# Forgetting attention with a gated feed-forward block: queries and keys of the first four pairs loaded in two parts, under a new load plan

## The chip, the cores and the metric

One core of a Trainium2 chip runs the whole program. The metric is the time of one execution in microseconds (us), as the device measures it; lower is better. A profile of one such execution stands beside it. Its engines are named as in the profile: PE (TensorE; PEld for its weight loads), DVE (VectorE), ACT (ScalarE), POOL (GpSimd), SP (SyncE, which issues transfers here). An engine's name with a q (SPq) is its queue of instructions that are not counted as busy, such as the issue of a transfer.

## The reference

Eight batches, eight heads, 576 positions of 64 numbers. Attention with a learned decay comes first, then a gated feed-forward block (FFN below) over the 4608 tokens:

```python
scores = scale * np.matmul(q, k.transpose(0, 1, 3, 2))          # 8 x 8 x 576 x 576
cum = np.cumsum(np.log(np.clip(f, 0.0001, 1.0)), axis=-1)
scores = np.where(causal, -1e9, scores + cum[..., :, None] - cum[..., None, :])
attn = np.exp(scores - np.max(scores, axis=-1, keepdims=True))
attn = attn / (np.sum(attn, axis=-1, keepdims=True) + 1e-09)
x = (attn @ v)  # as (4608, 512), heads side by side
g = x @ w_gate                                                  # 512 x 1536
return ((g / (1 + np.exp(-g))) * (x @ w_val)) @ w_out           # 1536 x 512
```

Inputs and output are float32. The kernel multiplies in bf16.

## The kernel before

**Pairs.** Two heads of one batch make a pair; there are 32, four to a batch. For a pair, k and q are loaded (L409), cast to bf16 (L434 to L438, on ACT, DVE or POOL), transposed on PE (L452) and copied out of PSUM into `kt` and `qz` (L464 on ACT, L466 on DVE); the copies below are named by these lines. `qz` holds a block of 64 rows of both heads beside zeros, so that one matmul makes 128 rows: 64 of each head.

**Groups.** The nine blocks of 64 rows of a pair are worked off in two groups: g0 is blocks 0 to 3 (rows 0 to 255), g1 is blocks 4 to 8. Group g0 needs only the first 256 rows of q and k. For each block PE makes scores (L498) and adds the causal mask (L502); DVE adds the summed gates `cb` and takes a row minimum (L526: "the add" below); ACT takes the exponential with its row sum (L546); the reciprocal is L564; POOL multiplies by it (L582). For the first eight pairs PE transposes the result (L612) and DVE or ACT copies it (L617); for later pairs a transposing transfer does that. PE multiplies with v (L638), and ACT or DVE copies the result into `xT` (L662), a ring of 2560 tokens.

**Gate sums.** `f` is loaded for all 64 heads (tile `t`, L364), clamped, its logarithm taken, and summed along the row by a DVE scan (L369). The sums are written to DRAM (`cum_f`, L378), and for each pair two transfers read two rows back, each spread over 64 partitions (L418, `cb`). Only pair 0 (`NSEL = 1`) gets its sums without DRAM: a float32 matmul with a 0/1 matrix `one` spreads them (L393, two halves of 288 columns), and ACT or DVE copies them (L397).

**FFN.** Tokens are taken in tiles of 256, 256, then seven of 512, then 256, 128, 128. For a tile, PE computes gate and value (L720) in units; a unit fills two PSUM banks. ACT takes tanh (L726), DVE multiplies twice (L728, L731). The tiles of 256 tokens have six units of 2 x 8 matmuls of 256 columns. The output projection is L748. Units are taken in a fixed order, so unit 0 of tile 0 needs the weight pieces wg0 and wv0, unit 1 wg2 and wv2, units 2 and 3 wg4 and wv4, units 4 and 5 wg8 and wv8 (the number is the first block of 128 columns that the piece holds). A tile needs `xT` of all four pairs of its batch for its tokens: tile 0 the g0 of pairs 0 to 3, tile 1 their g1, tile 2 the last rows of batch 0 and most of batch 1 (pairs 4 to 7).

**Order.** A planner in Python runs while the program is built. It lists every operation with a cost, an engine or a choice of engines and a priority, simulates the engines, and emits the operations in the order of their simulated starts; every engine then works through its queue in that order. `COLD` is the simulated time in ns up to which PE work is costed at double. `HEAD` gives the first units of work as pair and group; each later pair runs g1, then g0. `STARTUP` is the order of the first transfers, written by hand: `p2` stands for k and q of pair 2, `c2` for its gate sums from DRAM, `f9` for f, `v01` for piece 1 of v of batch 0 (128 rows of all heads), `wg4` for a weight piece (issued by POOL, cast on the way). Each entry waits for the landing of the one `AHEAD` places before it. `NUDGE` shifts priorities of single pairs, tiles or loads (`a4.1:1`: scores of pair 4, g1, later by one).

Of the kernel before, what the change touches and what calls it, by code (L numbers as in the profile page):

```python
# [13 lines left out]

BIG = 1.0e9
HUGE = 3.0e38
COLD = 25000
SLOW = 1.03


# [179 lines left out]
def kernel(  # L200
# [11 lines left out]
    nc = tc.nc  # L212
# [32 lines left out]
    JFROM = 8  # L245
    TWO = True
    NDIRECT = 0
    NSEL = 1
    MOST = (("p", 1), ("o", 2), ("f", 3))
    AHEAD = 7  # L250
    BEHIND = 6
    BOTH = 8
    LATER = {"DVE": 100}
# [3 lines left out]
    SOON = 8  # L257
    BACK = 4
    CBACK = 5
    STARTUP = "p0 f9 p1 c1 p3 p2 c2 v00 c3 wv0 wg2 wg0 wv2 v04 wv4 v01 v03 c4 wg4 v02 p4 wg8 wv8 v10 f0 p5 p6 c5 v14 c6 wo0 p7 wo4 v12 v13 v11 c7 wo8"  # L260
    HEAD = "10 00 20 30 11 01 31 21"


    NUDGE = "a10.0:1 a13.0:2 a15.0:-1 a15.1:-0.5 a16.1:-2 a20.0:-1 a21.0:1 a23.1:-1 a26.1:0.5 a27.1:-1.5 a28.0:1 a29.0:1 a31.1:10 f3:-4 f4:-7 f5:1 f6:2 f7:4.5 f8:4 f9:8 o6:-2.5 o8:2 q11:-2 q15:4 q22:5.5 q24:2.5"

    WAIT = ""
    ORDER = [(int(u[0]), int(u[1])) for u in HEAD.split()]
# [10 lines left out]
    def bufs(name, shape, dtype, n, space=None):  # L278
        pl.pool(name, [(space or sb).tile(shape, dtype, name=f"{name}{x}") for x in range(n)])
# [16 lines left out]
    bufs("qz", [P, NB, 2, QB], BF16, 4)  # L296
    bufs("cb", [P, S], F32, 5)
    bufs("t", [P, S], F32, 4)
    bufs("cm", [P, NB, QB], F32, 2)
# [7 lines left out]
    for n in ("pk", "pT"):  # L307
        both[n] = [sb.tile([P, sum(NSL), P], BF16, name=f"{n}{x}") for x in range(2)]
        pl.pool(n + "1", [x[:, 0:NSL[1], :] for x in both[n]])
        pl.pool(n + "0", [x[:, NSL[1]:, :] for x in both[n]])  # L310
    bufs("vf", [P, H, D], F32, 2)
    bufs("vt", [P, 5, H, D], BF16, 2)
    bufs("th", [P, 512], F32, 3)
    bufs("hh", [P, 512], BF16, 18)
# [21 lines left out]
    one = sb.tile([BH, 2 * max(NSEL, 1), 64], F32)  # L336
    setup({"POOL": 160 + 110 * NSEL}, lambda e: nc.gpsimd.tensor_copy(one, ident[0:BH, 0:2 * max(NSEL, 1)].unsqueeze(2).to_broadcast((BH, 2 * max(NSEL, 1), 64))),
          ["one"], -140)
    setup({"DVE": 100}, lambda e: nc.vector.memset(tiny, 1.0), ["tiny"], -300)
    pl.op({"ACT": 1400}, lambda e: nc.scalar.activation(tiny[:, 1:2], tiny[:, 0:1], AF.Ln), ["tiny"], ["ln"], -99.85)  # L340
# [33 lines left out]
    for p in range(NDIRECT):  # L374
# [5 lines left out]
    pl.op({"ACT": 1400}, lambda e: nc.scalar.activation(tiny[:, 1:2], tiny[:, 0:1], AF.Exp),  # L380
          [(("cb", p), 2) for p in range(NDIRECT)] + [("fa", 2), "ln"], ["exp"], -95)


    def select(p):
        pl.key(("cb", p), "cb", p)
        for n in range(2):
            a, z = S // 2 * n, S // 2 * (n + 1)
            bk = ("cs", p, n)
            pl.key(bk, "gv", line="c")

            def mult(e, p=p, bk=bk, a=a, z=z):
                w = one[:, 2 * p:2 * p + 2, :].rearrange("b h r -> b (h r)")
                nc.tensor.matmul(pl.buf(bk)[:, 0:z - a], w, pl.buf("fa")[0:BH, a:z], start=True, stop=True)  # L393
            pl.op({"PE": mm(4 * (z - a))}, mult, [("fa", 3), "one"], [bk], -98.5 + 3 * p, lat=220, holds=["fa"])

            def evac(e, p=p, bk=bk, a=a, z=z):
                (nc.scalar.copy if e == "ACT" else nc.vector.tensor_copy)(pl.buf(("cb", p))[:, a:z], pl.buf(bk)[:, 0:z - a])  # L397
            pl.op({"ACT": 370, "DVE": 385}, evac, [bk], [("cb", p), (("cb", p), 3)], -98.5 + 3 * p)

    def half(key):  # L400
        return pl.buf(key).bitcast(BF16)
# [2 lines left out]
    def load_pair(p):  # L404
        b, hp = divmod(p, NPB)
        s = first[p]
        for name, src, pr in (("k", k, 0), ("q", q, .1)):
# [5 lines left out]
        if NDIRECT <= p < NSEL:  # L413
            select(p)
        elif p >= NSEL:
            pl.key(("cb", p), "cb", p)
            for h in range(2):
                loads["cb", p, h] = pl.op({"SP": 600}, lambda e, h=h: nc.sync.dma_start(  # L418
                    out=pl.buf(("cb", p))[64 * h:64 * h + 64, :],
                    in_=cum_dram[2 * p + h:2 * p + h + 1, :].to_broadcast((64, S))),  # L420
                    ["cum_dram"], [("cb", p), (("cb", p), 3)], -98.5 + 3 * p if p < NPB else s - SOON + .2, dma=570, after=[sums[p - CBACK, 0 if p - CBACK >= NPB else 1]] if p >= NPB + 1 else [])

    def prepare(p):
        s = first[p]
        for name in ("k", "q"):
            fk, bk = (name + "f", p), (name + "b", p)
            KR, KC = ROWS[name]
            pl.key(bk, name + "b")

            def cast(e, name=name, fk=fk, bk=bk, KR=KR):  # L430
                src = pl.buf(fk)[0:KR, :, :].rearrange("p h (r d) -> p r h d", d=D)
                dst = pl.buf(bk)[0:KR, :, :, :]
                if e == "ACT":
                    nc.scalar.activation(dst, src, AF.Copy, scale=-scale if name == "q" else 1.0)  # L434
                elif name == "q":
                    eng[e].tensor_scalar(dst, src, -scale, 1.0, op0=ALU.mult, op1=ALU.mult)  # L436
                else:
                    eng[e].tensor_copy(dst, src)  # L438
            engs = {"POOL": 850 if p < 8 else 800 if name == "k" else 1010}
            if p < NPB:  # L440
                engs = {"POOL": 850, "ACT": 850, "DVE": 500} if name == "k" else {"POOL": 1050, "ACT": 1050, "DVE": 680}
            o = pl.op(engs, cast, [fk], [bk], s - 1 + (name == "q") * .1)
            o.bias = SPARE if p else {}
            tk = ("tt", name, p)
            pl.key(tk, "tx", line="q")
            ok = ("kt", p) if name == "k" else ("qz", p)
            pl.key(ok, ok[0])

            def transpose(e, bk=bk, tk=tk, KR=KR, KC=KC):
                src = pl.buf(bk).rearrange("p r h d -> p r (h d)")  # L450
                for j in range(KC):
                    nc.tensor.transpose(half(tk)[:, KR * j:KR * j + KR], src[0:KR, j, :], ident[0:KR, 0:KR])  # L452
            pl.op({"PE": KC * (KR / 2.4 + 2.5)}, transpose, [bk], [tk, ok], s - 1, lat=200)
            halves = [(0, P, None)] if name == "k" else [(0, 64, 0), (64, 128, 1)]
            for a, z, h in halves:
                def evac(e, a=a, z=z, h=h, tk=tk, ok=ok, KC=KC):
                    if h is None:
                        src = half(tk)[a:z, 0:S].rearrange("r (j p) -> r p j", j=KC)
                        dst = pl.buf(ok)[a:z, :].rearrange("r (p j) -> r p j", j=KC)
                    else:  # L460
                        src = half(tk)[a:z, 0:S].rearrange("r (j i p) -> r i p j", j=KC, i=NB)
# [6 lines left out]
                o.bias = LATER if p >= 8 else {}  # L468

    def epool(i):  # L470
        return f"e{i}" if i % 2 == 0 else "eo"

# [12 lines left out]
    def scores(p, g):  # L485
# [3 lines left out]
        for n, bank in enumerate(BANKS[g]):  # L489
# [11 lines left out]
                    if last and p < MFROM:  # L501
                        nc.tensor.matmul(sp[:, o - QB:o], ident, mask, start=False, stop=True)  # L502
            cols = [z - a for _, a, z in bank] + [64 for i, a, z in bank if z == QB * (i + 1) and p < MFROM]
            pl.op({"PE": mm(*cols)}, mult, [("kt", p), ("qz", p), (("kt", p), "done"), (("qz", p), "done"), "mask"], [sk], pr, lat=220)
            o = 0
            cuts = []
            for i, a, z in bank:
# [5 lines left out]
            for i, a, z in cuts:  # L513
# [265 lines left out]
    for x in STARTUP.split():  # L779
        n = int("".join(c for c in x if c.isdigit()))  # L780
        if x == "f9":
            line.append(loads["f", "fa", 0])
        elif x[0] == "f" and n < NDIRECT:
            line += [loads["f", ("cb", n), h] for h in range(2)]
        elif x[0] == "p":
# [84 lines left out]
```

## Time and profile before

| | |
|---|---|
| time, three runs | 419.38, 420.01 (median), 426.64 us |
| the profiled execution, its own time | 420.02 us |
| its span, first to last instruction | 418.2 us |
| PE busy | 398.1 us (95%) |
| DVE, ACT, POOL busy | 325.3, 311.0, 252.6 us (78%, 74%, 60%) |
| moved by DMA | 72.22 MB, mean 173 GB/s |

Busy time counts an engine's own instructions. A matmul's end is modelled, so a busy PE need not be a PE at its peak. The time outside the span is 420.02 - 418.2 = 1.8 us. A chain of waits is followed back from the last instruction, at each step to whatever released it. A window view gives the busy time of each engine in one stretch, with the number of its instructions as x. Sizes of transfers in the profile are those at the destination: 288 KB for k or q of a pair, 144 KB for a `cb` half or for f, 256 KB for a full piece of v, 256 or 512 KB for a weight piece.

### The profile page before, as it was taken

To read this page: it belongs to the slowest core of one execution; us is meant where nothing else is said; L and a number is where in the kernel's file an instruction comes from. 1 tells how busy PE (TensorE), PEld (TensorE's weight loads), DVE (VectorE), ACT (ScalarE), POOL (GpSimd) and SP (SyncE) were. 2 spreads that over 40 slices of the span, in tenths; PEclk is the share of its full clock that TensorE was granted. 3 is DMA by queue.
4 is the path that set the end of the run, shared out by engine and by line. 5 is a ranking of instruction groups with operands and counts; after the bars stand their busy time and mean duration, and the time that the engine had idled before them with its cause. 6 is when DMAs were issued, how large, how long until landed. Compare 5 with 4: busy or idle time off the path is not lost.

```text
span 418.2 us, 9999 instructions
## 1 busy us (share of the span) xinstructions
PE 398.1 (95%) x3304; PEld 231.8 (55%) x3304; DVE 325.3 (78%) x1044; ACT 311.0 (74%) x875; POOL 252.6 (60%) x460
## 2 busy tenths in 40 slices
PE   1679999999999999999999999999999999999996
PEld 1446887665555555555555555555454444447875
DVE  4589999989998979889998979898866474553532
ACT  4689999999999978888987979899886332223321
POOL 7399977999788983886795787759784000000000
PEclk9999999999999999999999999999999999999999
DMA  7999999997999999999999999979976401001111
GB/s 176 203 166 235 220 214 206 224 236 183 204 229 212 232 197 237 204 237 199 225 216 226 228 235 210 234 189 208 221 155 146 88 2 51 25 27 50 52 52 52
DMA packets 143029, 72.22 MB, mean 173 GB/s; under 512 B 117761, under 2 KB 129793, under 8 KB 142977
## 3 DMA queue, kind: packets, MB, share of 16 engines
q1 hardware_dynamic: 136804, 66.27, 73.8%
q0 software_dynamic: 5808, 4.72, 7.7%
q10 hardware_dynamic: 364, 0.59, 0.6%
q8 instruction: 26, 0.43, 0.4%
q14 instruction: 27, 0.21, 0.2%
HBM read 47.04 MB, written 9.58 MB: 135 GB/s over the span
## 4 chain that ended last, share of the span: by engine, by line
PE 77%; DMA 7%; ACT 6%; POOL 4%; DVE 3%; issue 2%; SPq 0%; POOLq 0%; DVEq 0%; ACTq 0%
PE gv L720 38%; PE gv L748 20%; PE sp L498 8%; PE tx L638 5%; DMA kf<-in_k_dram 3%; PE tx L452 3%; POOL pk L582 3%; PE gv L612 2%; DMA pT<-pk 2%; DVE t L526 2%; ACT eo L546 2%; ACT e L546 2%; PE sp L502 1%; DMA cb<-cum_f 1%; DMA cum_f<-t 1%
## 5 line engine op out<-in xcount | busy, mean ns | idle before, releaser
L526 DVE CUSTOM_DVE_ANT_0 t<-sp,cb 128x512 f32<-128x512 f32 (+7 forms) x288 | 130.9, 475 | 13.5 <-PE sp L502 5.0
L582 POOL TENSOR_SCALAR pk<-e,lr 128x128 bf16<-128x128 f32 (+3 forms) x190 | 100.1, 530 | 32.7 <-DVE lr L564 15.1
L720 PE MATMUL gv<-xT,wv 128*128 128x512 bf16 (+2 forms) x576 | 111.4, 326 | 0.0
L720 PE MATMUL gv<-xT,wg 128*128 128x512 bf16 (+2 forms) x576 | 111.3, 326 | 0.0
L728 DVE SCALAR_TENSOR_TENSOR th<-th,gv 128x512 f32<-128x512 f32 x108 | 73.9, 685 | 43.7 <-ACT th L726 43.2
L748 PE MATMUL gv<-wo,hh 128*128 128x512 bf16 (+1 forms) x444 | 107.5, 374 | 0.0
L726 ACT ACTIVATE th<-gv 128x512 f32<-128x512 f32 x108 | 64.0, 592 | 42.1 <-PE gv L720 40.3
L546 ACT ACTIVATE e<-t,tm 128x448 f32<-128x448 f32 (+4 forms) x160 | 88.5, 555 | 4.6 <-DVE tm L526 3.9
L731 DVE TENSOR_TENSOR hh<-th,gv 128x512 bf16<-128x512 f32 x108 | 73.4, 685 | 9.0 <-PE gv L720 5.5
L498 PE MATMUL sp<-kt,qz 128*128 128x448 bf16 (+6 forms) x320 | 72.8, 295 | 3.8 <-DVE tm L526 3.7
L582 POOL TENSOR_SCALAR pk<-eo,lr 128x256 bf16<-128x256 f32 (+3 forms) x128 | 67.7, 530 | 12.4 <-DVE lr L564 4.9
L546 ACT ACTIVATE eo<-t,tm 128x256 f32<-128x256 f32 (+3 forms) x128 | 71.2, 557 | 4.3 <-DVE tm L526 2.2
L720 PEld LDWEIGHTS <-wv 128*128 128x128 bf16 x576 | 49.3, 98 | 34.8
L720 PEld LDWEIGHTS <-wg 128*128 128x128 bf16 x576 | 49.2, 98 | 35.0
L748 PEld LDWEIGHTS <-hh 128*128 128x128 bf16 x444 | 39.7, 98 | 37.1
L502 PE MATMUL sp<-mask,ident 128*128 128x64 bf16 x288 | 48.2, 197 | 0.0
L755 ACT ACTIVATE ot<-gv 128x512 f32<-128x512 f32 (+1 forms) x33 | 19.1, 581 | 36.7 <-PE gv L748 34.7
L498 PEld LDWEIGHTS <-qz 128*128 128x128 bf16 x320 | 31.0, 101 | 19.8 <-DVE qz L466 1.3
L436 POOL TENSOR_SCALAR qb<-qf 72x1024 bf16<-72x1024 f32 x30 | 31.2, 1041 | 8.8 <-DMA qf<-in_q_dram 6.1
L502 PEld LDWEIGHTS <-ident 128*128 128x128 bf16 x288 | 27.2, 100 | 15.2 <-issue 3.9
L546 ACT ACTIVATION_READ_ACCUMULATOR e<-t,tm 128x1 f32 x160 | 30.7, 192 | 0.0
L638 PE MATMUL tx<-pT,vt 128*64 128x320 bf16 (+4 forms) x448 | 29.4, 266 | 0.7 <-DMA pT<-pk 0.3
(60 smaller groups left out, 379.7 us busy)
## 6 DMA issues: line engine op xcount, KB each, us to landing
out_dram<-ot SPq DMA_DIRECT2D x35, 256.0 KB
kf<-in_k_dram SPq DMA_DIRECT2D x31, 288.0 KB
qf<-in_q_dram SPq DMA_DIRECT2D x31, 288.0 KB
cb<-cum_f SPq DMA_DIRECT2D x62, 144.0 KB
vf<-in_v_dram SPq DMA_DIRECT2D x32, 256.0 KB
wo<-in_moe_w_out_dram POOLq DMA_DIRECT2D x3, 512.0 KB, 9.2
vf<-in_v_dram SPq DMA_DIRECT2D x8, 128.0 KB
wv<-in_moe_w_val_dram POOLq DMA_DIRECT2D x2, 512.0 KB, 8.3
```

Source lines behind the costliest of these rows:

```text
L436: eng[e].tensor_scalar(dst, src, -scale, 1.0, op0=ALU.mult, op1=ALU.mult)
L498: nc.tensor.matmul(sp[:, o:o + z - a], qz[:, i, :, :].rearrange("p h r -> p (h r)"), kt[:, a:z], start=True, stop=not last or p >= MFROM)
L502: nc.tensor.matmul(sp[:, o - QB:o], ident, mask, start=False, stop=True)
L526: nc.vector.tensor_tensor_reduce(out=pl.buf(tk)[:, a:z], in0=pl.buf(sk)[:, o:o + z - a], in1=pl.buf(("cm", p))[:, i, :] if own else pl.buf ...
L546: nc.scalar.activation(pl.buf(ek)[:, :L], pl.buf(tk)[:, :L], AF.Exp, bias=pl.buf(("tm", p, g))[:, 0, i:i + 1], scale=-1.0, accum_out=pl.bu ...
L582: eng[e].tensor_scalar(dst, src, r, 1.0, op0=ALU.mult, op1=ALU.mult)
L638: nc.tensor.matmul(xo[r, 0:QB * n], vt[:, c, 2 * hp + h, :], pT[:, a:a + n, 64 * h:64 * h + 64], start=(c == 0), stop=(c == nch - 1))
L720: nc.tensor.matmul(pl.buf(bk)[:, j * n:j * n + n], wt[:, ko, fc * P:fc * P + P], xT[:, ko, x0:x0 + n], start=ko == 0, stop=ko == KD - 1)
L726: pl.op({"ACT": 487}, lambda e, u=u: nc.scalar.activation(pl.buf(("th", t, u)), pl.buf(("wg", t, u)), AF.Tanh, scale=0.5), [("wg", t, u)], ...
L728: pl.op({"DVE": 605}, lambda e, u=u: nc.vector.scalar_tensor_tensor(pl.buf(("th", t, u)), pl.buf(("th", t, u)), 1.0, pl.buf(("wg", t, u)), ...
L731: pl.op({"DVE": 605}, lambda e, u=u: nc.vector.tensor_mul(pl.buf(("hh", t, u)), pl.buf(("th", t, u)), pl.buf(("wv", t, u))), [("u", t, u), ...
L748: nc.tensor.matmul(pl.buf(bk)[:, 0:z - a], hh[:, (fc % nf) * n + ms * P:(fc % nf) * n + ms * P + P], wo[:, fc, a:z], start=fc == 0, stop=f ...
```

## The change

- For the first four pairs (`NHALF = 4`) q and k come in parts. Part A is rows 0 to 255 of two pairs together (pairs 0 and 1, pairs 2 and 3), on 128 partitions, 64 for each pair: one cast and four transposes of 128 columns for both. Part B is rows 256 to 575: k for two pairs together (128 partitions, five transposes), q for each pair alone (80 partitions, four transposes). Each pair's share is a transfer of its own. The copies out of PSUM are made for each pair and part. The part A transfers of pairs 0 and 1 are issued by ACT, the others by SP.
- The gate sums are split at the same row. PE spreads part A for all four pairs (`NSELA = 4`) and part B for pair 0. Pairs 1 to 3 read only part B from DRAM.
- The g0 scores and adds of these pairs wait for parts A only.
- `HEAD` begins with pair 0 instead of pair 1.
- `STARTUP`, `AHEAD` (7 to 10), `NUDGE` and `COLD` (25000 to 31000) are new; in `STARTUP` `p0` and `p2` now are parts A of two pairs, `k0`, `k2` and `q0` to `q3` parts B. `vf`, which v lands in, has three buffers instead of two; the unused `cm` is gone. The table load for the exponential is put off by a penalty on ACT.

```diff
-COLD = 25000
+COLD = 31000
...
+    NHALF = 4
+    NSELA = 4
     NSEL = 1
+    CUT = QB * (HI[0] + 1)
-    AHEAD = 7
+    AHEAD = 10
...
-    STARTUP = "p0 f9 p1 c1 p3 p2 c2 v00 c3 wv0 wg2 wg0 wv2 v04 wv4 v01 v03 c4 wg4 v02 p4 wg8 wv8 v10 f0 p5 p6 c5 v14 c6 wo0 p7 wo4 v12 v13 v11 c7 wo8"
-    HEAD = "10 00 20 30 11 01 31 21"
-    NUDGE = "a10.0:1 a13.0:2 a15.0:-1 a15.1:-0.5 a16.1:-2 a20.0:-1 a21.0:1 a23.1:-1 a26.1:0.5 a27.1:-1.5 a28.0:1 a29.0:1 a31.1:10 f3:-4 f4:-7 f5:1 f6:2 f7:4.5 f8:4 f9:8 o6:-2.5 o8:2 q11:-2 q15:4 q22:5.5 q24:2.5"
+    STARTUP = "p0 f9 c0 v01 p2 wv0 v00 q1 q0 k0 c1 wg2 wv2 wg0 q2 k2 c3 q3 v02 wg8 wv4 v04 v03 c2 wg4 wv8 c5 p4 v10 p5 p6 p7 v14 c4 wo8 wo0 v11 c7 c6 wo4 v12 v13"
+    HEAD = "00 10 20 30 01 11 21 31"
+    NUDGE = "a2.1:2 a4.1:1 a8.0:1 a17.0:2 a20.0:2 a22.1:-1 a24.0:-0.5 a25.1:1 a27.1:-1.5 f4:1.5 f5:9 f8:6 o0:5.5 o4:-4 q18:4 q22:3 q26:-0.5 q28:-3.5 q29:-2.5"
...
-    bufs("vf", [P, H, D], F32, 2)
+    bufs("vf", [P, H, D], F32, 3)
...
+    def select(p, part, a, z):
+        bk = ("cs", p, part)
+        pl.key(bk, "gv", line="c")
+        def mult(e):
+            w = one[:, 2 * p:2 * p + 2, :].rearrange("b h r -> b (h r)")
+            nc.tensor.matmul(pl.buf(bk)[:, 0:z - a], w, pl.buf("fa")[0:BH, a:z], start=True, stop=True)
...
+    def parts(p):
+        if p % 2 == 0:
+            yield "k", "A", 0, CUT, 4, 2
+            yield "q", "A", 0, CUT, 4, 2
+            yield "k", "B", CUT, S, 5, 2
+        yield "q", "B", CUT, S, 4, 1
+
+    def load_parts(p):
...
+                for u in range(n):
+                    h0 = 2 * (hp + u)
+                    (nc.scalar if e == "ACT" else nc.sync).dma_start(
+                        out=pl.buf(fk)[m * u:m * u + m, :, 0:r * D],
+                        in_=src[b, h0:h0 + 2, a:z].rearrange("h (p r) d -> p h (r d)", r=r))
...
+        for x, a, z, sel in (("A", 0, CUT, NSELA), ("B", CUT, S, NSEL)):
+            if p < sel:
+                select(p, x, a, z)
+                continue
+            for h in range(2):
+                loads["cb", p, x, h] = pl.op({"SP": 600}, lambda e, h=h, a=a, z=z: nc.sync.dma_start(
+                    out=pl.buf(("cb", p))[64 * h:64 * h + 64, a:z],
+                    in_=cum_dram[2 * p + h:2 * p + h + 1, a:z].to_broadcast((64, z - a))),
+                    ["cum_dram"], [(("cb", p), x)], -98.5 + 3 * p, dma=z - a, holds=[("cb", p)])
...
-            pl.op({"PE": mm(*cols)}, mult, [("kt", p), ("qz", p), (("kt", p), "done"), (("qz", p), "done"), "mask"], [sk], pr, lat=220)
+            pl.op({"PE": mm(*cols)}, mult, pair_done(p, g) + ["mask"], [sk], pr, lat=220, holds=[("kt", p), ("qz", p)])
...
-                r = [sk, ("cm", p) if own else (("cb", p), 3)] + ([("m", p, i, "part")] if a and not two else [])
+                r = [sk] + ([("cm", p)] if own else cb_done(p, g)) + ([("m", p, i, "part")] if a and not two else [])
```

More of the change, by code (lines that the diff above doesn't have):

```diff
@@ L298 @@
     bufs("t", [P, S], F32, 4)
-    bufs("cm", [P, NB, QB], F32, 2)
     for i in range(0, NB, 2):
@@ L335 @@
     tiny = sb.tile([P, 2], F32)
-    one = sb.tile([BH, 2 * max(NSEL, 1), 64], F32)
-    setup({"POOL": 160 + 110 * NSEL}, lambda e: nc.gpsimd.tensor_copy(one, ident[0:BH, 0:2 * max(NSEL, 1)].unsqueeze(2).to_broadcast((BH, 2 * max(NSEL, 1), 64))),
+    one = sb.tile([BH, 2 * NSELA, 64], F32)
+    setup({"POOL": 160 + 110 * NSELA}, lambda e: nc.gpsimd.tensor_copy(one, ident[0:BH, 0:2 * NSELA].unsqueeze(2).to_broadcast((BH, 2 * NSELA, 64))),
           ["one"], -140)
@@ L379, with evac, cb_done, pair_done @@
           [("fa", 3)], ["cum_dram"], -120, dma=570, lat=0, holds=["fa"])
-    pl.op({"ACT": 1400}, lambda e: nc.scalar.activation(tiny[:, 1:2], tiny[:, 0:1], AF.Exp),
+    o = pl.op({"ACT": 1400}, lambda e: nc.scalar.activation(tiny[:, 1:2], tiny[:, 0:1], AF.Exp),
           [(("cb", p), 2) for p in range(NDIRECT)] + [("fa", 2), "ln"], ["exp"], -95)
[L384 to L398, printed above, removed]
+    o.bias = {"ACT": 1000}
+    def select(p, part, a, z):
[4 more added lines that the diff above has]
+            nc.tensor.matmul(pl.buf(bk)[:, 0:z - a], w, pl.buf("fa")[0:BH, a:z], start=True, stop=True)
+        pr = at[p, 0] - 1.2 if part == "A" else at[p, 1] - 1
+        pl.op({"PE": mm(4 * (z - a))}, mult, [("fa", 3), "one"], [bk], pr, lat=220, holds=["fa"])
+        def evac(e):
+            (nc.scalar.copy if e == "ACT" else nc.vector.tensor_copy)(pl.buf(("cb", p))[:, a:z], pl.buf(bk)[:, 0:z - a])
+        pl.op({"ACT": (z - a) * .833 + 130, "DVE": (z - a) / .96 + 85}, evac, [bk], [("cb", p), (("cb", p), part)], pr)
+    def cb_done(p, g):
+        return [(("cb", p), x) for x in ("A", "B")[:g + 1]] if p < NHALF else [(("cb", p), 3)]
+    def pair_done(p, g):
+        if p >= NHALF:
+            return [("kt", p), ("qz", p), (("kt", p), "done"), (("qz", p), "done")]
+        return [(("kt", p), x) for x in ("A", "B")[:g + 1]] + [(("qz", p), x) for x in ("A", "B")[:g + 1]]
     def half(key):
@@ L406, in load_pair @@
         s = first[p]
+        if p < NHALF:
+            load_parts(p)
+            return
         for name, src, pr in (("k", k, 0), ("q", q, .1)):
@@ L412, in load_pair @@
                 (), [(name + "f", p)], (-99 + 3 * p if p < NPB else s - SOON) + pr, dma=1060, after=[sums[p - BACK, 0 if p - BACK >= NPB else 1]] if p >= NPB else [])
-        if NDIRECT <= p < NSEL:
-            select(p)
-        elif p >= NSEL:
+        if p >= NSEL:
             pl.key(("cb", p), "cb", p)
@@ L424, in prepare @@
         s = first[p]
+        if p < NHALF:
+            prepare_parts(p)
+            return
         for name in ("k", "q"):
@@ L468, in prepare, with load @@
                 o.bias = LATER if p >= 8 else {}
+    def parts(p):
[5 more added lines that the diff above has]
+    def load_parts(p):
+        b, hp = divmod(p, NPB)
+        pl.key(("cb", p), "cb", p)
+        for name, x, a, z, r, n in parts(p):
+            fk = (name + "f", p, x)
+            pl.key(fk, name + "f")
+            m = (z - a) // r
+            def load(e, fk=fk, src=(k if name == "k" else q), a=a, z=z, r=r, n=n, m=m):
+                for u in range(n):
[3 more added lines that the diff above has]
+                        in_=src[b, h0:h0 + 2, a:z].rearrange("h (p r) d -> p h (r d)", r=r))
+            loads[name, p, x] = pl.op({"ACT" if p == 0 and x == "A" else "SP": 550 * n}, load, (), [fk], -99 + 3 * p, dma=n * (z - a) * 2)
+        for x, a, z, sel in (("A", 0, CUT, NSELA), ("B", CUT, S, NSEL)):
[7 more added lines that the diff above has]
+                    ["cum_dram"], [(("cb", p), x)], -98.5 + 3 * p, dma=z - a, holds=[("cb", p)])
@@ new lines, in prepare_parts, with cast, transpose, evac @@
+    def prepare_parts(p):
+        for name, x, a, z, r, n in parts(p):
+            fk, bk, tk = (name + "f", p, x), (name + "b", p, x), ("tt", name, p, x)
+            m = (z - a) // r
+            pr = min(at[p + u, x == "B"] for u in range(n)) - 1 + (name == "q") * .1
+            pl.key(bk, name + "b")
+            pl.key(tk, "tx", line="q")
+            def cast(e, name=name, fk=fk, bk=bk, r=r, w=m * n):
+                src = pl.buf(fk)[0:w, :, 0:r * D].rearrange("p h (r d) -> p r h d", d=D)
+                dst = pl.buf(bk)[0:w, 0:r, :, :]
+                if e == "ACT":
+                    nc.scalar.activation(dst, src, AF.Copy, scale=-scale if name == "q" else 1.0)
+                elif name == "q":
+                    eng[e].tensor_scalar(dst, src, -scale, 1.0, op0=ALU.mult, op1=ALU.mult)
+                else:
+                    eng[e].tensor_copy(dst, src)
+            L = 2 * r * D
+            o = pl.op({"POOL": L + 60, "ACT": L * .833 + 210, "DVE": L * .62 + 60}, cast, [fk], [bk], pr)
+            o.bias = SPARE if p else {}
+            oks = [(("kt" if name == "k" else "qz"), p + u) for u in range(n)]
+            if x == "A":
+                for ok in oks:
+                    pl.key(ok, ok[0])
+            def transpose(e, bk=bk, tk=tk, r=r, w=m * n):
+                src = pl.buf(bk).rearrange("p r h d -> p r (h d)")
+                for j in range(r):
+                    nc.tensor.transpose(half(tk)[:, w * j:w * j + w], src[0:w, j, :], ident[0:w, 0:w])
+            pl.op({"PE": r * (m * n / 2.4 + 2.5)}, transpose, [bk], [tk] + (oks if x == "A" else []), pr, lat=200, holds=oks)
+            for u in range(n):
+                for lo, hi, h in ([(0, P, None)] if name == "k" else [(0, 64, 0), (64, 128, 1)]):
+                    def evac(e, lo=lo, hi=hi, h=h, u=u, tk=tk, ok=oks[u], a=a, z=z, r=r, n=n, m=m):
+                        src = half(tk)[lo:hi, 0:r * m * n]
+                        if h is None:
+                            src = src.rearrange("c (j u p) -> c u p j", j=r, u=n)[:, u, :, :]
+                            dst = pl.buf(ok)[lo:hi, a:z].rearrange("c (p j) -> c p j", j=r)
+                        else:
+                            src = src.rearrange("c (j u i p) -> c u i p j", j=r, u=n, i=(z - a) // QB)[:, u, :, :, :]
+                            dst = pl.buf(ok)[lo:hi, a // QB:z // QB, h, :].rearrange("c i (p j) -> c i p j", j=r)
+                        if e == "ACT":
+                            nc.scalar.copy(dst, src)
+                        else:
+                            nc.vector.tensor_copy(dst, src)
+                    pl.op({"ACT": (z - a) * .85 + 125, "DVE": (z - a) * 1.15 + 90}, evac,
+                          [tk] + ([("z", "qz", p + u)] if h is not None and p + u < len(pl.pools["qz"]) else []),
+                          [(oks[u], x)], at[p + u, int(x == "B")] - .9, holds=[oks[u]])
@@ L782 @@
             line.append(loads["f", "fa", 0])
+        elif x[0] == "p" and n < NHALF:
+            line += [loads["k", n, "A"], loads["q", n, "A"]]
+        elif x[0] in "kq":
+            line.append(loads[x[0], n, "B"])
+        elif x[0] == "c" and n < NHALF:
+            line += [loads["cb", n, y, h] for y in "AB" for h in range(2) if ("cb", n, y, h) in loads]
         elif x[0] == "f" and n < NDIRECT:
```

## The prediction

> **What bounds the kernel now.** I read the page's 40 slices first, then windows of the first 60 us, the chain of waits up to the first add, then the timeline where FFN tile 2 starts.
>
> ```profile
> PE   1679999999999999999999999999999999999996
> ```
>
> PE is short of work only in the first four slices (10.45 us each); from there to the end its digit is 9. So the end moves by what PE has done before it fills up. The windows show the first stretch (columns: window, its length, PE, PEld, DVE, ACT, POOL busy, clock, DMA share, GB/s):
>
> ```profile
> 5.00:10.00 5.00, 1.52 (x8) 1.24 (x9) 3.27 (x4) 3.11 (x4) 3.36 (x8) 1.00 0.79 191
> 10.00:15.00 5.00, 4.15 (x39) 2.95 (x38) 1.79 (x3) 2.90 (x5) 1.77 (x3) 1.00 0.82 214
> 15.00:20.00 5.00, 2.74 (x32) 2.20 (x30) 3.50 (x12) 2.55 (x9) 1.79 (x2) 1.00 1.17 211
> 20.00:25.00 5.00, 2.56 (x25) 2.16 (x24) 4.34 (x30) 4.71 (x20) 3.53 (x8) 1.00 1.43 164
> 25.00:30.00 5.00, 4.45 (x24) 2.29 (x24) 4.41 (x20) 4.60 (x18) 4.91 (x11) 1.00 0.92 156
> 30.00:35.00 5.00, 4.17 (x41) 2.29 (x41) 4.96 (x18) 4.59 (x16) 4.96 (x10) 1.00 1.16 210
> ```
>
> DVE and ACT are half idle up to 20 us and nearly full from 20 us on. What made them wait is the chain up to the first add (start, length, what):
>
> ```profile
> 1.38 6.10 DMA kf<-in_k_dram
> ...
> 8.81 3.11 DMA cum_f<-t
> ...
> 12.45 5.02 DMA cb<-cum_f
> ...
> 17.63 0.39 DVE t L526
> ```
>
> The gate sums exist at 7.80 us (scan at 6.45, 1.35 long); writing them to DRAM and reading them back for pair 1, first in order, costs until 17.63 us. The FFN starts with its tile 0 at 34.83 us and reaches tile 2 at 98.68 us:
>
> ```profile
> 34.83 1.03 PE L720 MATMUL gv<-xT,wg 128*128 128x256 bf16 x8
> 98.68 1.03 PE L720 MATMUL gv<-xT,wg 128*128 128x512 bf16 x4
> ```
>
> The windows of L720 alone show 3.99 us in 70 to 80, none in 80 to 90 and 8.49 in 100 to 110. The units of tiles 0 and 1 were used up by about 80 us, and PE got by on projections and attention until batch 1 was through. So up to 98 us it is the attention, on DVE and ACT together, that sets the pace, and PE after it.
>
> That DVE and ACT share one load can be worked out. Engine time of one pair among the first eight, from the groups of instructions, both engines summed: exponentials (88.5 + 71.2)/32 = 4.99; adds (130.9 + 8.8)/32 = 4.37; k and q copies (24.5 + 13.2 + 18.9 + 8.3)/32 = 2.03; copies of transposed weights (11.8 + 9.9)/8 = 2.71; copies into xT (17.2 + 7.2)/32 = 0.76; sums and reciprocals (11.4 + 6.1 + 5.2)/32 = 0.71. Sum 15.57 us. An FFN unit takes (64.0 + 73.9 + 73.4)/108 = 1.96. Batch 0 and six units: 4 x 15.57 + 6 x 1.96 = 74.0, by two engines 37.0 us; from 17.63 that ends at 54.6. Its last L638 starts at 54.82. The two engines explain the pace.
>
> **The change, part by part.**
>
> First add. The DRAM trip leaves the path of g0. A select of 288 columns takes 2.29/2 = 1.15 us, so one of 256 takes 1.02; a copy takes 0.40; with 0.2 between, sums ready at 7.8 are added from 9.5. PE can have transposes in front: up to 11.5. I take 10. Parts A must be there by then: before, whole 288 KB loads of k and q of pair 0 were cast from 5.63 and 7.84; now four transfers of 128 KB come in their place, issued by ACT in about 4 x 0.5 us, which delays its first table load from 1.87 to about 3; its logarithm starts only at 5.74, so that is hidden. If it were not, the delay would be about 1 us.
>
> What the earlier start is worth. Not 17.63 - 10 = 7.6 us: DVE and ACT did some of that time's copies and casts, and must still. Worth is what they idled: over 10 to 30 us, 3.21 + 1.50 + 0.66 + 0.59 = 5.96 on DVE and 2.10 + 2.45 + 0.29 + 0.40 = 5.24 on ACT, 11.2 together, **-5.6 us** for two engines. From 5 to 10 us they idled 1.73 and 1.89 more, worth up to 1.8; I count none of it, for the gates' chain holds both there. Lower bound: PE must fit four selects (4.1), pair 0's part B (1.28) and scores of four g0 (0.9 each, 18.54 to 19.44) after 7.8, about 9 us: the last g0 add at 17.5 instead of 25.47. PE fits it, at half pace if it must; if only half of the idle time is filled, -2.8.
>
> Work added to DVE and ACT. Selects: 4 copies of 256 and one of 320 columns against two of 288: by slope from 288 (0.40) and 576 (0.63), 4 x 0.375 + 0.425 - 0.80 = +1.1. Copies of k and q: six for a pair instead of three, 3 x (0.375 + 0.425) - 3 x 0.63 = +0.51, four pairs +2.0. Casts: at ACT's 1.04 us for 1024 elements, (512 + 512 + 640 + 2 x 512) x 1.016 ns = 2.73 for two pairs against 2 x (0.84 + 1.04) = 3.76, -2.1 for four. Net +1.1, **+0.55 us**. The selects' extra 768 columns cost PE 3.05 us, while it would stand idle (8.5 us before 8.48); without that cover, 3 us. `one` is four times as wide: 0.29 us on POOL becomes perhaps 0.6, done by 3 us, needed at 7.8.
>
> Transfers. Eight more from SP, at about 0.45 us of issue (0.58, 0.57, 0.44 at the start): 3.6 us on SP. Before, SP held three v issues for 9.65 us from 15.64, so there is room; a third `vf` takes that wait away. Without room they would delay weights by as much.
>
> Order of loads. In KB at the destination, up to and with the named load, before and now: wg0 4336 and 3504; v01 5488 and 912; wg4 6544 and 6640; p4 7376 and 8016; c4 6032 and 10416. Adding up GB/s of the windows, 4655 KB had moved by 25 us, 6485 by 35, 8895 by 45, 10965 by 55. Landings follow that with a lag of 2 to 5 us (wg0: issued 21.85, landing 5.7 later). So wg0 lands near 22 and v is early: tile 0 can start when its g0 is through, 34.83 - 7.4 = about 27.5. But units 2 and up need wg4, which comes at 41 us as before, and pair 4 can't add before c4, near 56 us; before, its scores stood at 48.43. Both queue: PE's scores of pair 4 fill both `sp` banks and wait, and DVE's next add waits behind them.
>
> The hole. Now batch 0 and units 0 and 1 need (4 x 15.57 + 3.9 + 1.1)/2 = 33.6 us from 10: done at 43.6. From 43 to 56, DVE and ACT have 26 engine-us. Units 2 to 9, one per 1.75 us of PE, offer 8 x 1.96 = 15.7; k and q copies of pairs 4 to 7 8.1; 23.8 in all. About 2.2 idle, plus what wg4 leaves open, against 1.5 before (40 to 60 us). I take 2.5 engine-us, **+1.25 us**; bounds 0, if c4 is earlier than I think, and 7.5 (below).
>
> Priorities (`NUDGE`, `COLD`) reorder work, remove none; no row prices them. The spread of PE's idle time after 60 us (0.30 + 0.34 in 60 to 80, 0.41 in 210 to 230) gives -1 to +3; I take 0.
>
> Sum: 420.0 - 5.6 + 0.55 + 1.25 = **416.2 us**. It stands against the profiled 420.02, which agrees with the median 420.01; the 1.8 us around the span stay. Its own range is 413 to 419.
>
> **Rivals.** (a) *Hidden anyway.* The start is earlier, but batch 1 is not: from pair 4's scores (48.43) to tile 2 (98.68) it took 50.2 us, with eight units in it (7.8 us). If those now lie before, tile 2 starts at 56 + 50.2 - 7.8 = 98.4, and the end is as before: 419.8. For it: c4's place. Against: of those 50.2 us, 31.1 are batch 1's own; the rest is later pairs' work, which would be done all the same.
>
> (b) *Slower: the c4 stall.* If the FFN units do not fill the wait for c4, since wg4 and wv8 come late too and PE stands in order behind pair 4's scores, the whole 56 - 48.4 = 7.6 us is lost at tile 2: 427.5. It begins to decide when c4 lands more than about 51 us + the earlier start's 5 = 56 us. Against: the planner can emit units before pair 4's scores.
>
> (c) *More.* No hole (-1.25), the idle of 5 to 10 us used (-1.8), and PE's clock up earlier. Mask matmuls of 64 columns took 0.26 us until 29.04 and 0.19 from 30.03 on, after PE had been close to full from 25 us: so it runs at half pace before. If the selects and g0 scores bring that forward, DVE and ACT wait less for PE (3.9 + 2.1 + 1.1 + 0.7 engine-us charged to PE in the first 35 us; half cured is 2.0 us): 411.2. The Trainium skill ("TensorE: Matmul & The Clock Gate", Part 1) has the gate open after about 3.4 us of sustained activity; by that rule selects and scores back to back from 8 us would open it near 12. Against: 4.15 busy us in 10 to 15 did not.
>
> (d) That parts A don't free g0: excluded by `pair_done` and `cb_done`; v and weights are early enough. It falls under (a).
>
> **How the numbers follow.** Forecast 0.48, (a) 0.20, (b) 0.20, (c) 0.12. The range 410 to 425 takes in (c), (a) and the smaller half of (b). About 2% (411.6 to 428.4) is what a measurement of this kernel can tell from no change: faster 0.12 from (c), slower 0.09 from (b) with nudges against it, the rest within.
>
> **What would show it.** First add near 10 us, no `cb` transfer in the chain before it; L393 about 5.3 us; first L720 near 27.5 (26 to 31); third unit not before 41; pair 4's first add near 56; tile 2's first 512-column matmul near 95. A first add later than 12, or tile 2 later than 98, makes the forecast wrong.

## The result, and the profile after

The changed kernel takes 423.65 us (median of 20 runs, 421.81 to 426.98); the kernel before took 420.68 in 20 runs. The ratio is 1.0063, 95% interval 1.0042 to 1.0085: 0.6% slower, where 0.9% faster was forecast. The medians given for the kernel before include a few disturbed runs, which the ratios leave out. The profiled execution took 423.48 us, its span 421.6.

The page's slices of PE, then windows of the first 60 us (columns: window, its length, PE, PEld, DVE, ACT, POOL busy, clock, DMA share, GB/s):

```profile
PE   0979799999999999999999999999999999999996
```

```profile
5.00:10.00 5.00, 0.61 (x4) 0.34 (x4) 2.24 (x3) 2.82 (x5) 3.48 (x5) 1.00 1.23 251
10.00:15.00 5.00, 4.75 (x22) 3.03 (x23) 0.69 (x3) 2.21 (x6) 3.88 (x6) 1.00 1.03 222
15.00:20.00 5.00, 5.00 (x29) 3.00 (x26) 4.52 (x24) 4.24 (x19) 2.05 (x5) 1.00 0.89 186
...
40.00:45.00 5.00, 2.57 (x40) 1.90 (x34) 4.22 (x16) 3.99 (x10) 3.12 (x5) 1.00 1.23 196
45.00:50.00 5.00, 4.38 (x35) 3.02 (x36) 1.76 (x5) 2.10 (x5) 0.83 (x2) 0.67 1.03 224
```

The start is earlier: DVE and ACT are nearly full from 15 us on, not from 20. But a new hole stands at 42 to 50 us, where the kernel before was full: DVE and ACT together are busy 3.86 of 10 engine-us in 45 to 50. The chain of waits to 62 us names it, and the timeline shows both ends, the issue on POOL and the matmul that waits:

```profile
34.17 11.40 DMA wg<-in_moe_w_gate_dram
```

```profile
34.17 0.80 POOL L791 DMA_DIRECT2D wg<-in_moe_w_gate_dram  x1
...
45.62 1.05 PE L816 MATMUL gv<-xT,wg 128*128 128x256 bf16 x8 [3.00 <-DMA wg<-in_moe_w_gate_dram]
```

L816 is the old L720. This is the first matmul of unit 2 of tile 0, which needs wg4. In the new `STARTUP` wg4 stands behind wg8 and wv4, though wg8 is not needed before unit 4. PE worked in order, so its attention work stood behind that matmul too: the transposes of pair 4's q came at 48.54 us, not 45.23. In the timeline DVE stands idle for it:

```profile
47.80 0.49 DVE L758 CAST xT<-tx 128x320 bf16<-128x320 f32 x1 [3.58 <-PE tx L734]
```

Tile 2 starts 4.0 us later than the 98.68 before, and the span is 3.4 us longer:

```profile
102.67 1.03 PE L816 MATMUL gv<-xT,wg 128*128 128x512 bf16 x4
```

### The profile page after: what moved, and what is told of

The parts are those of the page before. It is cut to its first block, busy times and chain, and to the rows that moved or that the text cites. A ratio compares the mean times of both kernels' runs of the same rounds, so it can differ in the third digit from the quotient of the medians.

```text
span 421.6 us, 9959 instructions
## 1 busy us (share of the span) xinstructions
PE 399.1 (95%) x3247; PEld 233.2 (55%) x3296; DVE 324.1 (77%) x1057; ACT 314.8 (75%) x880; POOL 252.0 (60%) x459
## 4 chain that ended last, share of the span: by engine, by line
PE 88%; DMA 4%; DVE 3%; POOL 2%; issue 2%; ACT 1%; ACTq 0%; DVEq 0%; POOLq 0%
PE gv L816 42%; PE gv L844 22%; PE sp L594 9%; PE tx L734 6%; PE tx L467 3%; DMA wg<-in_moe_w_gate_dram 3%; PE sp L598 2%; PE gv L708 1%; PE gv L395 1%; DMA kf<-in_k_dram 1%; POOL pk L678 1%; DVE t L622 1%; PE tx L546 1%; DVE pT L713 0%; DVE t L373 0%
## 5 line engine op out<-in xcount | busy, mean ns | idle before, releaser
L678 POOL TENSOR_SCALAR pk<-e,lr 128x512 bf16<-128x512 f32 (+3 forms) x189 | 99.9, 532 | 56.0 <-DVE lr L660 20.3
L816 PE MATMUL gv<-xT,wg 128*128 128x512 bf16 (+2 forms) x569 | 110.7, 325 | 3.4 <-DMA wg<-in_moe_w_gate_dram 3.0
L816 PE MATMUL gv<-xT,wv 128*128 128x512 bf16 (+2 forms) x558 | 108.9, 325 | 1.5 <-DVE qz L561 0.8
L844 PE MATMUL gv<-wo,hh 128*128 128x512 bf16 (+1 forms) x422 | 102.6, 373 | 1.3 <-issue 0.2
L642 ACT ACTIVATE e<-t,tm 128x320 f32<-128x320 f32 (+4 forms) x160 | 88.7, 556 | 3.8 <-DVE tm L622 3.4
L594 PE MATMUL sp<-kt,qz 128*128 128x64 bf16 (+7 forms) x318 | 73.0, 295 | 1.0 <-DVE tm L622 0.6
L816 PEld LDWEIGHTS <-wg 128*128 128x128 bf16 x576 | 48.9, 98 | 37.1 <-DMA wg<-in_moe_w_gate_dram 3.3
L816 PEld LDWEIGHTS <-wv 128*128 128x128 bf16 x576 | 49.5, 98 | 34.4
L734 PE MATMUL tx<-pT,vt 128*64 128x320 bf16 (+4 forms) x448 | 30.3, 269 | 1.1 <-ACT qz L559 0.6
L451 POOL TENSOR_SCALAR qb<-qf 72x1024 bf16<-72x1024 f32 x28 | 29.1, 1040 | 2.8 <-DMA qf<-in_q_dram 1.2
```

What stands on the lines that cost most here:

```text
L594: nc.tensor.matmul(sp[:, o:o + z - a], qz[:, i, :, :].rearrange("p h r -> p (h r)"), kt[:, a:z], start=True, stop=not last or p >= MFROM)
L642: nc.scalar.activation(pl.buf(ek)[:, :L], pl.buf(tk)[:, :L], AF.Exp, bias=pl.buf(("tm", p, g))[:, 0, i:i + 1], scale=-1.0, accum_out=pl.bu ...
L678: eng[e].tensor_scalar(dst, src, r, 1.0, op0=ALU.mult, op1=ALU.mult)
L734: nc.tensor.matmul(xo[r, 0:QB * n], vt[:, c, 2 * hp + h, :], pT[:, a:a + n, 64 * h:64 * h + 64], start=(c == 0), stop=(c == nch - 1))
L816: nc.tensor.matmul(pl.buf(bk)[:, j * n:j * n + n], wt[:, ko, fc * P:fc * P + P], xT[:, ko, x0:x0 + n], start=ko == 0, stop=ko == KD - 1)
L844: nc.tensor.matmul(pl.buf(bk)[:, 0:z - a], hh[:, (fc % nf) * n + ms * P:(fc % nf) * n + ms * P + P], wo[:, fc, a:z], start=fc == 0, stop=f ...
```

## The experiments

Where the text says "plan kept", the planner's list of operations is that of the kernel named, operation for operation, and the edit works on that list. Otherwise the planner made a new plan, in which anything may move. Each group of runs has its own runs of the kernel before beside it, with medians from 420.4 to 422.0 us; so kernels of different groups are compared by their ratios to it, and differences in us between groups are rough.

**wg4 and wg8 traded, plan kept.** Theory 1: the late wg4 makes the loss. Theory 2: the loss is in the extra copies and the new priorities.

```diff
-        for o in pl.order():
+        done = pl.order()
+        x, y = loads["wg", 4], loads["wg", 8]
+        x.fn, y.fn = y.fn, x.fn
+        for o in done:
```

> The changed kernel with its plan kept instruction by instruction; only the weight pieces wg4 and wg8 trade their places of issue on POOL (25.25 and 34.17 us). Theory 1, the late wg4 makes the loss: PE no longer waits for a weight transfer (3.00 us before the 45.62 matmul), its clock does not fall behind it, tile 2 starts near 99 instead of 102.67, time 3 to 4 us lower, 419.5 to 420.5. Theory 2, the loss is in the extra copies and the new priorities and the wait only fills slack: the time stays within 1 us of 423.6.

Measured: 419.63 us (12 runs), ratio to the kernel before 0.9964 (0.9938 to 0.9989), 4.0 us below the changed kernel. Tile 2 starts at 99.20. The windows (columns as above) show the hole filled, and the timeline has the first add, 2.4 us before that of the kernel before:

```profile
40.00:45.00 5.00, 4.94 (x70) 3.83 (x67) 4.99 (x18) 5.00 (x13) 3.27 (x5) 1.00 1.25 192
45.00:50.00 5.00, 4.84 (x55) 4.14 (x52) 4.67 (x15) 4.94 (x14) 4.44 (x7) 1.00 1.02 236
```

```profile
15.26 0.42 DVE L622 CUSTOM_DVE_ANT_0 t<-sp,cb 128x256 f32<-128x256 f32 x1 [1.25 <-PE sp L598]
```

Two weight pieces in the wrong order are worth 4.0 us, more than the whole loss. Theory 2 falls.

**The same trade in the kernel before, plan kept.** It puts the fault into a kernel that had none.

> The kernel before with its plan kept; only wg4 and wg8 trade their places of issue (31.91 and 36.19 us). Theory 1: unit 2, which starts at 42.61, waits for wg4 until about 45.6, PE's queue stands behind it, time 2 to 3 us above the kernel before, 422 to 423. Theory 2: no change, 420.2.

Measured: 426.05 us (6 runs), ratio 1.0137 (1.0091 to 1.0183): 5.6 us more than the 420.4 beside it, about twice what was expected. The row of unit 2 in the timeline:

```profile
46.35 0.83 PE L720 MATMUL gv<-xT,wg 128*128 128x256 bf16 x6 [3.52 <-DMA wg<-in_moe_w_gate_dram]
```

It began at 42.61 before; tile 2 moved from 98.68 to 103.13, 4.45 us. The span less that start grew as well, from 319.5 to 320.7 us, and why it did was not followed. The price at tile 2 is larger than the wait that the row shows, which the filler run below is about.

**The logarithm and the scan ahead of the cast of k, plan kept.** The trace after gives a second place. In the timeline of ACT and DVE:

```profile
6.43 0.63 ACT L530 ACTIVATE kb<-kf 128x512 bf16<-128x512 f32 x1 [1.29 <-DMA kf<-in_k_dram]
6.96 0.67 ACT L372 ACTIVATE t<-t 64x576 f32<-64x576 f32 x1
```

```profile
8.43 1.67 DVE L373 TENSOR_TENSOR_SCAN t<-tiny,t 64x576 f32<-64x576 f32 x1
```

The clamped gates are ready at 4.81 us (DVE: 4.00 + 0.81), but ACT's queue has the cast of k's part A first, which waits for its transfer until 6.43; on DVE two copies of k stand ahead of the scan. Gate sums come at 10.10 us, not at 7.80 as before. The edit moves three operations:

```diff
+        done = [o for o in done if o not in (cast, ln, scan)]
+        at_ = max(done.index(clamp) + 1, 0)
+        start = min(n for n, o in enumerate(done) if o.start >= cast.start)
+        at_ = max(at_, start)
+        done[at_:at_] = [ln, cast, scan]
```

> The changed kernel with its plan kept, but the logarithm and the scan of the gates stand ahead of the cast of k's first part in ACT's and DVE's queues. Both theories: gate sums ready near 7.4 us instead of 10.1, first add near 13.3 instead of 14.83 (the copies of q's first part then end last). Theory 1: wg4 lands as late as now, so PE's wait at 42 us takes the gain back, time lower by 0.5 us at most. Theory 2, the head sets the end one to one: lower by 1.5 us, 422.1.

Measured: 421.72 us (12 runs), ratio 1.0020 (0.9992 to 1.0048), 1.9 us below the changed kernel. The scan ends at 7.09, the first add is at 12.53. wg4 was not as late as expected: POOL got to its issue at 31.87 instead of 34.17, so unit 2 began at 43.59. Theory 1's bound of 0.5 us was wrong for that reason; the wait itself is still there (3.3 us).

**Both edits.**

> Both edits: wg4 and wg8 trade places, and the logarithm and the scan go first. Theory 1: without the wait the head counts, so 0.5 to 1.5 us below the swap alone, 418 to 420. Theory 2: as the logarithm alone, about 422. A rival to both, that POOL and the elementwise engines are full from 20 us on: equal to the swap alone within 0.5 us.

Measured: 416.83 us (6 runs), ratio 0.9910 (0.9880 to 0.9939): faster than both kernels, 2.8 us below the trade alone. So with the wait gone the earlier start counts, by about twice what was expected of it, and the rival of full engines falls. First add and tile 2 in the timeline:

```profile
12.59 0.42 DVE L623 CUSTOM_DVE_ANT_0 t<-sp,cb 128x256 f32<-128x256 f32 x1 [1.25 <-PE sp L599]
```

```profile
95.65 1.03 PE L817 MATMUL gv<-xT,wg 128*128 128x512 bf16 x4
```

**Filler in PE's wait.** How much of the late wg4's price is the wait, how much the clock? The window of 45 to 50 us after shows a granted clock of 0.67. A narrower one shows half of full speed for 3.4 us:

```profile
46.70:50.10 3.40, 3.40 (x28) 2.24 (x28) 1.76 (x5) 2.19 (x5) 0.93 (x2) 0.50 0.93 227
```

The edit, in the changed kernel with its plan kept:

```diff
+                    if (t, u, nm) == (0, 2, "wg"):
+                        for _ in range(26):
+                            nc.tensor.matmul(pl.buf(bk)[:, 0:256], ident, xT[:, 0, 0:256], start=True, stop=True)
```

> The changed kernel with its plan kept; ahead of unit 2 of FFN tile 0, 26 matmuls of 256 columns (26 x 0.109 = 2.8 us at full clock) on data that is there run into the same bank and are overwritten. They fill PE's wait for wg4 and do nothing else. If the price of the late wg4 is mostly PE's clock, which drops to half for 3.4 us after the wait: the drop goes and the time falls by about 1.5 us, to 422. If it is the wait itself, PE's queue standing still: unit 2 still begins at 45.6 and the time stays within 0.5 us of 423.6.

In that run the loop variable was bound late, the condition never held and no filler was emitted: it ran the changed kernel's instructions again, in 424.80 us (12 runs), ratio 1.0073 (1.0041 to 1.0106), with unit 2 at 45.37 and tile 2 at 102.30. It is a repeat of the changed kernel and tests nothing of the clock. With the variable bound:

> The same edit as in the run before, with the loop variable bound, so that the 26 filler matmuls (2.8 us at full clock) really run in PE's wait for wg4 at 42.4 us. If the clock's drop after the wait is a good part of the late wg4's price: the drop (46.7 to 50.1 us) goes, unit 2 still begins near 45.6, the time falls by 1 to 2 us, to 422. If the price is PE's queue standing still: no change, 423.6 within 0.5 us.

Measured: 422.42 us (12 runs), ratio 1.0023 (0.9993 to 1.0054): 1.2 us below the changed kernel, 2.4 below the repeat; by the ratios 1.7 and 2.1. Timeline and window:

```profile
42.50 3.00 PE L816 MATMUL gv<-xT,ident 128*128 128x256 bf16 x26
```

```profile
45.00:50.00 5.00, 5.00 (x61) 3.99 (x60) 2.92 (x9) 3.41 (x8) 1.54 (x3) 1.00 1.02 225
```

Unit 2 began at 45.35, nearly as late as before, yet tile 2 at 100.81 instead of 102.67 (102.30 in the repeat). So 1 to 2 of the 4 us are clock lost after the wait. The share is not exact: in this profile the clock did not dip in 30 to 35 us either, as it did in the changed kernel's (0.70 there). That dip can't be worth much on PE, though, since PE reached the wait at 42.50 here and at 42.62 there.

**Part A of the gate sums through DRAM, plan of the version with both edits.** For pairs 1 to 3, the copy becomes two transfers and the select's matmul goes:

```diff
+            if p and part == "A":
+                for h in range(2):
+                    nc.sync.dma_start(out=pl.buf(("cb", p))[64 * h:64 * h + 64, a:z],
+                                      in_=cum_dram[2 * p + h:2 * p + h + 1, a:z].to_broadcast((64, z - a)))
+                return
```

> The version with both edits (logarithm first, wg4 and wg8 traded; 416.83 us), plan kept, but part A of the gate sums of pairs 1 to 3 is read from DRAM by SP instead of being spread by PE (three selects and copies fewer). If the spread on PE is what frees g0: the first add of pair 0 is earlier by one select (about 1.1 us), those of pairs 1 to 3 wait for the trip, tile 2 starts 1 to 3 us later than 95.65, time 418 to 420. If pair 0 covers the trip: within 0.5 us of 416.8, or below it for the selects saved. SP also stands still until the sums are written, which delays the loads behind.

Measured: 420.50 us (12 runs), ratio 0.9965 (0.9937 to 0.9993), against 0.9910 for the version with both edits. That is a loss of 3.7 us by the medians, 2.3 by the ratios (their intervals leave some 1.7 either way) and 3.3 by the profiled spans: 2 to 4 us. Pair 0 adds earlier, at 11.37; pair 1 waits:

```profile
18.23 0.43 DVE L630 CUSTOM_DVE_ANT_0 t<-sp,cb 128x256 f32<-128x256 f32 x1 [3.84 <-DMA cb<-cum_f]
```

It added at 15.52 with the spread; tile 2 moved from 95.65 to 98.86. The spread on PE is worth its matmuls. The run can't tell how much of that is the trip and how much SP's standing still for it.

**Planned anew, one part at a time.** Five more kernels, whose priorities were set for another plan. `NSELA = 1` in the changed kernel (the order in which the pairs take the `cb` buffers is changed with it):

> The changed kernel with NSELA = 1, planned anew: PE spreads the gate sums of pair 0 alone, pairs 1 to 3 read part A from DRAM too (six more transfers of 64 KB, three selects fewer). If the spread on PE is what frees g0: adds of pairs 1 to 3 begin only after the sums' trip, near 17.5 us or later, and tile 2 starts 1 to 3 us later than in the changed kernel, time 424 to 427. If the DRAM trip is hidden behind pair 0 and q's copies: 422 to 424. A new plan can move wg4 too; tile 2's start says which.

Measured 435.55 us (4 runs; 1.0336, 1.0290 to 1.0382): the second group of adds begins at 21.03, behind copies of q on DVE, and the third at 31.47, after a wait of 2.29 us for a `cb` transfer. `NSEL = 4` in the kernel before, `cm` left out:

> The kernel before with NSEL = 4 and without the unused cm (for room), planned anew: PE spreads all gate sums of pairs 0 to 3, nothing else of the change. If the spread alone brings the start: first add near 12 to 13 us instead of 17.63, limited by the copies of whole q; tile 2 near 96 to 98, time 417 to 420. If the parts are needed for it: first add not before 15 and 420 to 422.

Measured 429.27 us (4 runs; 1.0183, 1.0130 to 1.0236), above both theories: the eight selects stand in one row in PE's queue, 8.05 us from 9.10, ahead of q's transposes, and the first add comes at 20.45. Without the parts the spread stands in its own way. `HEAD = "00 10 20 30 01 11 21 31"` in the kernel before:

> The kernel before with HEAD beginning at pair 0, whose gate sums PE spreads, planned anew. The first add no longer waits for the trip through DRAM: near 12.5 to 14 us. If four pairs' sums are needed for the start to count, the next pair waits for DRAM as before and tile 2 stays within 1 us of 98.7, time 419 to 421. If the first pair's start counts: 1 to 2 us less.

Measured 431.61 us (4 runs; 1.0245, 1.0199 to 1.0290): first add at 14.09, near what was expected, but tile 2 at 102.57 and then the end 327 us after it (319.5 in the kernel before). wg4 before wg8 in `STARTUP`, planned anew:

> The changed kernel with wg4 and wg8 traded in STARTUP and everything planned anew from it, with the priorities as they were. Theory 1 (a late wg4): unit 2 begins by 42.5 us as in the traded plan, time near 419.6. The priorities were set for the other plan, so the later order can differ by some us either way; tile 2's start tells that apart from the wait.

Measured 424.28 us (10 runs; 1.0068, 1.0032 to 1.0104). Unit 2 begins at 39.83, so the wait for wg4 is gone, and still tile 2 starts at 101.06: the new plan lost elsewhere what the trade won. Among its waits is one for another weight:

```profile
PE gv L844 <- DMA wo<-in_moe_w_out_dram: 1.4, 1, 1.4
```

That wait does not account for 4 us, and where the rest went was not followed. Last, the old order of loads put into parts:

```diff
+    STARTUP = "p0 f9 c0 p2 q1 k0 q0 c1 k2 q3 q2 c2 v00 c3 wv0 wg2 wg0 wv2 v04 wv4 v01 v03 c4 wg4 v02 p4 wg8 wv8 v10 p5 p6 c5 v14 c6 wo0 p7 wo4 v12 v13 v11 c7 wo8"
```

> The changed kernel with the old order of loads put into parts (gate and value weights as before: wv0 wg2 wg0 wv2 wv4 wg4 wg8 wv8; v after q and k), planned anew. The parts without the new load plan. If the parts are sound and the load plan is at fault: no wait of PE for weights, tile 2 at 98 or before, time 417 to 421. If the parts need their own order: v01 or wg0 late, first FFN matmul after 34, time above 423.

Measured 428.48 us (4 runs; 1.0172, 1.0123 to 1.0220): first add at 12.93, but the first FFN matmul only at 39.62. The parts need a load plan of their own. Of these five, the starts of adds and units can be read; the times mix in the plan.

## Why the prediction was wrong

**What sets the end: right for one plan.** The end follows the start of tile 2. In the kernels that keep the changed kernel's plan, span less that start is 418.1 - 99.20 = 318.9, 419.5 - 100.59 = 318.9, 414.6 - 95.65 = 318.9, 419.7 - 100.81 = 318.9, 417.9 - 98.86 = 319.0; in the changed kernel itself 318.9. Under another plan it is another number: 319.5 in the kernel before, 327.1 with its new `HEAD`. Behind tile 2 the new plan gained 0.6 us, where the prediction took 0 for the priorities.

**Order of loads: the step that failed.** The prediction put wg4 at 41 us "as before", since its place in bytes is nearly the same (6640 KB for 6544). It was ready at 45.6. Bytes were the wrong measure: wg4 stood third among the big pieces instead of second, and POOL issued it at 34.17 instead of 31.91, behind normalizing work and casts that kept POOL busy; then it took 11.4 us to land (9.3 in the median of the two gate pieces of its size before). The planner's code also holds a weight piece back, in its simulation, until the piece two before it has landed: wv2 for wg4 before, wg8 now. Whether that condition set the place in POOL's queue is not shown. c4, which I feared, was no cause: SP issued it by 34.2 us, ahead of its place. Pair 4's first add came at 55.84, close to the 56 that I gave, but because PE stood in front of unit 2; with the trade it came at 51.15. So the hole was real, but with wg4 as its cause; it was priced at +1.25, and the trade measures 4.0.

**First add: mis-sized.** Predicted 10 (bounds 9.5 to 11.5), measured 14.83, past the 12 that I had named as making the forecast wrong. I looked at ACT's table load and not at the cast of k that stood before the logarithm in the same queue. Putting the gates first gives 12.59, still past the upper bound. The rest is q and the selects: with both edits q's part A was cast from 8.44, after its transfer, and transposed from 9.12, four copies on ACT took 1.51 us from 9.76, and the scores came at 11.66, behind two more selects.

**What the start is worth: mis-sized too.** The -5.6 counted all 11.2 engine-us that DVE and ACT idled in 10 to 30 us as filled. The same window before, after and with both edits:

```profile
10.00:30.00 20.00, 13.90 (x115) 9.61 (x115) 14.05 (x61) 14.76 (x50) 12.00 (x23) 1.00 1.08 186
10.00:30.00 20.00, 17.20 (x119) 11.02 (x120) 14.64 (x68) 15.51 (x57) 14.26 (x28) 0.99 0.99 193
10.00:30.00 20.00, 17.43 (x127) 10.93 (x127) 16.41 (x76) 16.95 (x60) 15.60 (x31) 0.93 1.12 223
```

DVE and ACT still idle 9.85 engine-us after and 6.64 with both edits. Counted as the prediction counts, the start was worth 0.7 and 2.3 us, not 5.6. One term was left out: the 9 us of PE work up to the last g0 scores held no transposes. With both edits PE took 12.3 us for that stretch, from 7.92 to 20.2, and 3.9 us of it are transposes. So the last g0 add came at 24.20, and at 21.95 with both edits, where 17.5 was named; the first FFN matmul came at 32.96 and 30.63, where 27.5 was.

With both edits the measured time is 416.83, beside a forecast of 416.2, and tile 2 starts at 95.65, where 95 was forecast. The two faults, 4.0 and 2.8, make up 6.8 of the 7.4 us between forecast and result. That the sum comes so close is partly luck: by that count the start gave 3.3 us less than forecast, and in its place no hole was left (0.57 engine-us idle in 40 to 60 us, against 1.51 before), DVE and ACT idled less in 60 to 95 us (2.80 against 4.22), and 0.6 us came after the start of tile 2.

**The selects on PE: right in their sign.** L395 took ten matmuls of 0.68 us in the median against four before. They were costed at nothing beyond their copies, on the ground that PE would stand idle; PE was busy 9.75 of 10 us in 10 to 20 us, and with three selects fewer pair 0's first add came 1.2 us earlier. By the DRAM run they are worth 2 to 4 us all the same.

**Rivals.** The mechanism of (b), FFN units that do not fill the wait because weights are late and PE's queue stands behind them, is what happened, with wg4 in c4's place and half the price: I had made c4's landing the condition, which was not it. (a) fits the numbers of the trade alone, which came to 419.63 us and tile 2 at 99.20, where (a) has 419.8 and 98.4. Both edits refute it: c4 keeps its place in the order, the first add moves from 15.26 to 12.59, and tile 2 moves 3.55 us with it, so the start is not hidden. In (c) the clock did rise earlier, but to fall again. Masks took 0.19 us from 24.55 on, not from 30.03, and 0.26 again from 30.53 to 34.01; the windows show 0.96 in 25 to 30 and 0.70 in 30 to 35 after. A rise near 12 us did not come: masks still took 0.26 at 22.20, after those 9.75 busy us.

## What to carry to other kernels

In a plan with an order written out by hand, check for each large load not only how many bytes stand before it, but which instruction on its issuing engine stands before it, and what stands behind its first user; an in-order engine that waits for a weight holds up all other work in its queue. Keep the plan and trade two transfers before you judge a larger change: here two lines decided whether a sound idea was 0.6% slower or, with one more repair, 0.9% faster. And a parameter changed under a planner changes everything after it: the same trade was worth 4.0 us with the plan kept and nothing with a new plan.

## What the runs showed of the hardware

After a wait of 3.0 us, PE ran at half clock for 3.4 us (0.50 in 46.70 to 50.10); with the wait filled by useless matmuls, it did not. The same drop followed the wait of 3.52 us in the traded kernel before (0.51 in 47.50 to 51.00). The Trainium skill ("TensorE: Matmul & The Clock Gate", "Why this matters for your kernels") asks for no PE gaps over some 3 us between bursts; these two waits agree. But in the repeat the drop followed a wait of 2.70 us (0.51 in 45.30 to 48.70), and in the changed kernel the clock also fell with no such wait before it:

```profile
29.50:33.50 4.00, 3.89 (x30) 2.38 (x30) 3.09 (x11) 3.80 (x11) 4.00 (x8) 0.57 1.20 239
```

PE's longest wait in the five us before was 0.63 us; it was busy 2.65 us in 25.0 to 29.5. Nor is the first rise fixed: in four runs with the same order of work on PE up to 40 us, masks fell to 0.19 us at 17.85, 24.55, 24.83 and 27.68. The clock column doesn't show the first cold stretch: it reads 1.00 for the kernel before in 25 to 30 us, while masks of 64 columns still took 0.26 us up to 29.04.

A POOL cast that meets the DVE scan is stretched beyond the scan's end. In the timeline of POOL, after and with both edits, the same cast:

```profile
8.87 1.64 POOL L534 CAST kb<-kf 128x512 bf16<-128x512 f32 x1
```

```profile
9.02 0.60 POOL L535 CAST kb<-kf 128x512 bf16<-128x512 f32 x1
```

The first began during the scan of 8.43 to 10.10 and ended 0.4 us behind it; the second ran after a scan that had ended at 7.10. The scan took 1.67 us there against 1.35. The trade alone shows the same pair: scan 1.76 us, cast 1.64, ending 0.4 us behind it. The Trainium skill ("SBUF — State Buffer", Terms) says that the two engines share a pair of ports, which one of them holds for a whole instruction; the stretched cast fits that; the longer scan is not explained by these rows.
